# Attention with a decaying complex state and a gated layer on one core: slope clamp dropped, phase turns of two units rounded on ScalarE, new positions for many steps

## The chip, the cores and the metric

The kernel runs on one core of a Trainium2 chip. That core has TensorE (PE; PEld is its weight load), VectorE (DVE), ScalarE (ACT), GpSimd (POOL) and SyncE (SP), whose queue issues nearly all DMAs here. The metric is the device time of one execution in microseconds (us), lower is better.

## The reference

For every batch `b` (4), head `h` (8) and step `t` (768) a 48 x 48 state is turned and decayed by a complex number per row, a product of `k` and `v` is added to its real part, and `q` reads it. The result, 3072 tokens of 384 numbers, goes through a gated layer of width 2048.

```python
mag = np.sqrt(a_re * a_re + a_im * a_im)
scale = np.minimum(mag, 0.999) / (mag + 1e-06)
...
    new_re = ar * S_re - ai * S_im
    new_im = ar * S_im + ai * S_re
    S_re, S_im = (new_re + kv, new_im)
    y[:, :, t] = np.einsum('bhd,bhde->bhe', q[:, :, t], S_re)
...
h = x @ w_in
sp = np.where(h > 20.0, h, np.log1p(np.exp(np.minimum(h, 20.0))))
g = h * np.tanh(sp)
return (g @ w_out).astype(np.float32)
```

## The kernel before, in words

**Units.** The tokens are cut into 12 units of 256 steps (three to a batch), a unit into two chunks of 128. Each unit goes through three stages.

**Elementwise (`ew_steps`).** From `a_re` and `a_im` (tiles `R`, `I`) come the running log magnitude (a scan on DVE, line 333) and the running phase (scans, line 347). The slope `I = a_im * X1` (line 306) is clamped to -1.5..1.5 (line 307), and `test` (line 312) counts whether every ratio is small enough; if not, a flag at the end sends the program to a general path. The phase is brought to one turn in `phi2`: the number of turns `n` as an integer (line 352, DVE), then a subtraction (line 353). ScalarE's exponentials (line 123) and arctangents and sines (line 143) need two tables, so `with_trig` fences the second kind between two table loads (line 131). `grow` multiplies `q` and `k` by the magnitudes (POOL for most units), `rot` by cosine and sine (line 397), and `relay` sends the results through 12 small DMAs per unit from SP into tiles `T` with heads side by side (line 388). Tile `T` has three buffers, one per chunk. Units 0 and 1 work on one chunk at a time, later units on both at once.

**Attention (`attn_steps`), chunk by chunk on PE.** `pkn` transposes the keys (ScalarE copies them to `kn`, line 460), `pa` multiplies keys by queries (DVE masks it into `am`, line 470), `ypsum` gathers `am` times `V` and the old state, `pd` is the chunk's addition to the state (DVE, lines 501 and 503), and `S` times the chunk's last magnitude ends the update (line 505, DVE in unit 0, then POOL). ScalarE copies `ypsum` to `y` (line 488), four DMAs `xf<-y` (line 516) turn it, and `split` makes `xH` and `xL` of it.

**Gated layer (`moe_steps`).** Per pair `j` of eight, 18 matmuls `ph` (line 543), a chain of four activations and DVE steps from `e` to `gh` and `gl`, and later 12 matmuls `po` (line 571). Every product is made of three, with high and low parts of both sides. The weights come in as 64-bit numbers and are converted on the way in 24 pieces of 512 columns (`convert`): ScalarE takes the low words (line 123, `raw<-raw` or `wraw<-wraw`), DVE builds the high words (lines 190 and 194), POOL adds (line 199), ScalarE or DVE copies the high part (line 157) and DVE subtracts (line 158). Pieces named `raw` become `wi`, pieces named `wraw` become `wo`.

**Order.** Each step has a position in the plan, counted in pairs (`EW`, `AT`, `WP`, `LD` for loads, `MB` for the two halves of the layer; `ES`, `TS`, `WS` shift the priority against the position). A scheduler takes the steps by these numbers and lays down one fixed order per engine, and each engine and SP's queue then work strictly in that order. `after` and the numbers `CGA`, `CGN`, `LG` add edges: here the low words of the weights must follow certain trigonometric activations, and `LG = -1` makes the loads of unit 2 wait for the last relay of unit 1. `warm` issues 18 matmuls on a mask (`junk`, line 432) as soon as the first phase is there.

Of the kernel before, what the change touches and what calls it, by code (L numbers as in the profile page):

```python
# [14 lines left out]
F32 = mybir.dt.float32  # L15
# [15 lines left out]
UNITS = B * NU  # L31
# [5 lines left out]
NPAIR = DF // (2 * P)  # L37
# [5 lines left out]
GATE = -1  # L43
GRP = 2
RG, QG, GN = 5, 1, 0
SQ0, SORD, CGA, CGN, CGD, ACTG = 1, 0, 3, 3, 0, 0
YDVE = []
RQ = [(), ()]
LG, WG = -1, 12
W1 = 0  # L50
ADDV = 12
CLAMPP, MAGP = 0, 0
ROTU = 2
ROTP = [2]
# [12 lines left out]
FAST = [0, 1]
EW = [(-16.31, -10.95), (-12.73, -8.83), (-13.6, -11.78), (-17.21, -10.84), (-16.32, -10.6)]
AT = [(-7.75, -4.28), (-4.18, -0.81), (-7.43, -2.2), (-9.42, -3.06), (-10.26, -2.73)]
WP = [(-7.98, -3.45), (-3.03, 2.5), (2.11, 8.49), (9.4, 9.68)]  # L70
WS = [-3.58, -0.64, -1.09, 0.24]
ES = [2.49, -0.99, -0.86, 1.6]
TS = [-0.14, -1.22, 2.46, -0.05]
MB = [-1.35, -0.11]
WL1 = -1.83
RB = 2
XB = 2
LD = [(-17.86, -16.7, -16.5), (-19.19, -20.26, -20.22), (-17.97, -17.71, -17.6), (-21.41, -14.83, -16.39), (-24.18, -15.85, -17.38)]
WL = 512
XRUNS = ((0, 0, 0, 32), (0, 1, 32, 16), (64, 1, 64, 16), (0, 2, 80, 32))  # L80
LOW, HIGH, FADED = 0.55, 2e6, 1e-17
INV2PI = 1.0 / (2.0 * math.pi)
# [4 lines left out]
def tile_kernel(ctx, tc, q, k, v, are, aim, w_in, w_out, out):  # L87
    nc = tc.nc
# [3 lines left out]
    ew = ctx.enter_context(tc.tile_pool(name="ew", bufs=1))  # L92
# [74 lines left out]
    turned = []  # L167
# [13 lines left out]
    def convert(n, raw, dst, ws, raw_is_in=False):  # L181
        u = raw.bitcast(U32).rearrange("p (n two) -> p n two", two=2)
        lo, hi = u[:, :, 0], u[:, :, 1]
        if not TRUNC:
            ins = act(lo.bitcast(I32), lo, AF.Copy, scale=2.0 ** -29)
            if CGA < 9:
                after(ins, trig[0 if len(converted) < CGN else CGA])
            converted.append(ins)
        x = me.tile([P, ws], U32, tag="wx", name="wx", bufs=WXB)
# [40 lines left out]
    def ew_steps(u):  # L230
# [51 lines left out]
        def alloc():  # L282
            if u == 0:
                st["X1"] = at.tile(T4, F32, tag="y", name="X10", bufs=1)
                st["X"] = at.tile(X5, F32, tag="T", name="X0", bufs=TB)
            else:
                st["X1"] = ew.tile(T4, F32, tag="X1", name="X1", bufs=XB)
                st["X"] = ew.tile(X5, F32, tag="X", name="X", bufs=XB)

        def size(g):  # L290
# [13 lines left out]
        def slope(g):  # L304
            R, I, X1, x2, x3 = get(g)
            (nc.gpsimd if 0 < u <= MULP else nc.vector).tensor_tensor(I, I, X1, ALU.mult)
            (nc.gpsimd if 0 < u <= CLAMPP else nc.vector).tensor_scalar(I, I, -1.5, 1.5, ALU.max, ALU.min)
            act(x2, x2, AF.Ln, scale=4.0, bias=tiny)

        def test(g):  # L310
# [38 lines left out]
        def phi2(g):  # L349
            R, I, X1, x2, x3 = get(g)  # L350
            n = I.bitcast(I32)
            nc.vector.tensor_scalar(n, X1, INV2PI, None, ALU.mult)
            turned.append(nc.vector.scalar_tensor_tensor(I, X1, INV2PI, n, ALU.mult, ALU.subtract))
            if g != 0 and uu + 1 < NU:
                nc.vector.tensor_copy(ncar, st["I"][:, NCH - 1, :, C - 1])
# [81 lines left out]

    def attn_steps(u):
# [8 lines left out]
        def chunk(c):  # L447
# [26 lines left out]
            def yv(g):  # L474
                def f():
# [54 lines left out]
    def moe_steps(st, row0, unit=UNITS, cut=False, act=act):  # L530
# [29 lines left out]
        def mm2(j):  # L560
            def f():
# [30 lines left out]
    plan = []  # L592
# [9 lines left out]
    for u in range(NUN):  # L602
# [45 lines left out]
def general(tc, nc, q, k, v, are, aim, pools, moe_steps, split):  # L648
# [162 lines left out]
```

## Time and profile before

| | |
|---|---|
| median of 3 runs | 655.73 us (652.61 to 659.77) |
| profiled execution | 653.54 us, span 651.7 us, mean granted clock 0.944 |
| PE busy | 581.7 us, 89% of the span, 4468 matmuls |
| DVE busy | 502.1 us, 77% |
| ACT busy | 489.2 us, 75%, 45 table loads |
| POOL busy | 127.5 us, 20% |
| first attention matmul | 27.55 us |
| last matmul begins | 645.20 us |

The page cuts the span into 40 slices of 16.3 us. PE is at 9 tenths or more in nearly all slices from the thirteenth on, and mostly below that in the twelve before; the granted clock (PEclk) is below full speed only in those first twelve. A busy share is an average over stages with different limits, so the stages are read apart below.

### The profile page before, as it was taken

How to read it: one execution, taken by the hardware profiler on the slowest of the kernel's cores; microseconds unless marked ns; L12 is line 12 of the kernel's file. 1: busy time of each engine (PE TensorE's matmuls, PEld its weight loads, DVE VectorE, ACT ScalarE, POOL GpSimd, SP SyncE). 2: the span in 40 equal slices, each digit the busy share in tenths (PEclk: the TensorE clock that was granted, in tenths of full speed). 3: DMA queues.
4: the chain of work that ended last, by engine and by line, in shares of the span. 5: the costliest groups of instructions: out<-in, count | busy, mean ns of one | idle time of the engine just before them, and what ended most of it. 6: DMA issues, size and time to landing. Idle time of an engine off the chain costs nothing.

```text
span 651.7 us, 11747 instructions
## 1 busy us (share of the span) xinstructions
PE 581.7 (89%) x4468; PEld 554.5 (85%) x4468; DVE 502.1 (77%) x875; ACT 489.2 (75%) x785; POOL 127.5 (20%) x101
## 2 busy tenths in 40 slices
PE   0686956698689999999999999999999999999996
PEld 0475846598579999999989999999899999999995
DVE  6968989999848869878869868978788796544552
ACT  7857967797757778887988977977888878645661
POOL 2316257435201112002003003003012030000000
PEclk9856888599779999999999999999999999999999
DMA  8765723612840270260460530621711602201000
GB/s 303 219 238 142 245 82 101 190 33 85 210 144 13 87 191 5 89 179 1 117 153 25 143 101 26 183 63 29 192 49 49 171 2 83 64 26 25 1 26 29
DMA packets 58528, 67.05 MB, mean 103 GB/s; under 512 B 4960, under 2 KB 51040, under 8 KB 58464
## 3 DMA queue, kind: packets, MB, share of 16 engines
q1 hardware_dynamic: 58464, 66.23, 35.1%
q8 instruction: 37, 0.61, 0.4%
q14 instruction: 27, 0.22, 0.1%
HBM read 36.96 MB, written 5.51 MB: 65 GB/s over the span
## 4 chain that ended last, share of the span: by engine, by line
PE 38%; DVE 23%; ACT 18%; DMA 7%; issue 7%; SPq 5%; POOL 2%; DVEq 0%; POOLq 0%; ACTq 0%
PE ph L543 14%; PE po L571 13%; ACT e L123 6%; ACT L131 4%; PE pa L467 4%; PE ypsum L483 4%; DVE e L548 3%; DMA R<-a_re 3%; ACT X L123 3%; SPq L388 3%; DVE gl L158 3%; DMA T<-QK 3%; DVE X L347 2%; PE pd L497 2%; DVE R L333 2%
## 5 line engine op out<-in xcount | busy, mean ns | idle before, releaser
L571 PE MATMUL po<-wo,gh 128*128 128x384 f32 x768 | 221.0, 348 | 16.8 <-DVE wo L157 6.0
L543 PE MATMUL ph<-xH,wiH 128*128 128x256 f32 x576 | 169.3, 295 | 10.4 <-ACT xH L157 9.6
L543 PE MATMUL ph<-xL,wiH 128*128 128x256 f32 x576 | 167.3, 291 | 3.1 <-DVE xL L158 3.1
L543 PE MATMUL ph<-xH,wiL 128*128 128x256 f32 x576 | 167.7, 291 | 0.9 <-DVE wiL L158 0.9
L571 PEld LDWEIGHTS po<-wo,gh 128*128 128x128 f32 x768 | 141.6, 190 | 22.5 <-DVE wo L157 6.7
L123 ACT ACTIVATE e<-e 128x512 f32<-128x512 f32 x192 | 119.7, 629 | 50.8 <-DVE e L548 48.9
L571 PE MATMUL po<-wo,gl 128*128 128x384 f32 x384 | 131.3, 342 | 0.0
L543 PEld LDWEIGHTS ph<-xH,wiH 128*128 128x128 f32 x576 | 113.4, 197 | 14.4 <-ACT xH L157 10.4
L543 PEld LDWEIGHTS ph<-xL,wiH 128*128 128x128 f32 x576 | 113.4, 197 | 4.1 <-DVE xL L158 4.1
L543 PEld LDWEIGHTS ph<-xH,wiL 128*128 128x128 f32 x576 | 113.5, 197 | 1.1 <-DVE wiL L158 1.1
L505 POOL TENSOR_TENSOR S<-S,T 96x384 f32<-96x384 f32 x18 | 27.6, 1533 | 314.7 <-DVE S L503 110.3
L553 DVE SCALAR_TENSOR_TENSOR g<-e,ph 128x512 f32<-128x512 f32 x96 | 65.3, 680 | 22.2 <-ACT e L123 21.3
L548 DVE TENSOR_SCALAR e<-e 128x512 f32<-128x512 f32 x96 | 55.9, 583 | 31.5 <-ACT e L123 31.3
L158 DVE TENSOR_TENSOR gl<-g,gh 128x512 fp32r<-128x512 f32 x96 | 75.0, 781 | 1.6
L123 ACT ACTIVATE e<-ph 128x512 f32<-128x512 f32 x96 | 56.5, 591 | 24.6 <-PE ph L543 24.4
L571 PEld LDWEIGHTS po<-wo,gl 128*128 128x128 f32 x384 | 73.1, 190 | 0.4 <-issue 0.4
L123 ACT ACTIVATE e<-e,fifth 128x512 f32<-128x512 f32 x96 | 69.1, 720 | 1.8
L157 DVE CAST gh<-g 128x512 fp32r<-128x512 f32 x96 | 41.0, 427 | 34.3 <-PE po L571 32.6
L131 ACT ACT_TABLE_LOAD x45 | 57.7, 1283 | 1.6 <-PEq L767 0.8
L375 POOL TENSOR_TENSOR QK<-QK,X 128x1536 f32<-128x1536 f32 (+1 forms) x12 | 40.5, 3377 | 76.8 <-ACT X L123 73.2
L467 PE MATMUL pa<-T 96*128 96x128 f32 x384 | 52.9, 288 | 0.6 <-DVE am L470 0.6
L467 PEld LDWEIGHTS pa<-T 96*128 96x128 f32 x384 | 49.5, 203 | 1.2 <-DVE am L470 0.8
(89 smaller groups left out, 820.8 us busy)
## 6 DMA issues: line engine op xcount, KB each, us to landing
T<-X SPq DMA_DIRECT2D x72, 129.0 KB, 2.5
T<-QK SPq DMA_DIRECT2D x72, 129.0 KB, 3.3
raw<-w_in SPq DMA_DIRECT2D x12, 512.0 KB, 9.2
wraw<-w_out SPq DMA_DIRECT2D x12, 512.0 KB, 4.4
QK<-q SPq DMA_DIRECT2D x12, 384.0 KB, 4.3
QK<-k SPq DMA_DIRECT2D x12, 384.0 KB, 5.1
V<-v SPq DMA_DIRECT2D x12, 384.0 KB, 4.6
out_dram<-o SPq DMA_DIRECT2D x24, 192.0 KB, 1.9
```

What stands on the lines that cost most here:

```text
L123: ins = nc.scalar.activation(out, in_, func, **kw)
L131: ins = nc.scalar.preload_act_table_set(name)
L157: heng(h, src)
L158: leng(out=lo, in0=src, in1=h.bitcast(F32), op=ALU.subtract)
L375: (nc.vector if g in FAST and u == 0 else nc.gpsimd).tensor_tensor(QK[..., :C], QK[..., :C], X[..., :C], ALU.mult)
L467: nc.tensor.matmul(pa[:, i, :], st["T"][c][:, 4 * g + i, 1, :C], st["T"][c][:, 4 * g + i, 0, :C], start=True, stop=True)
L483: nc.tensor.matmul(py[64 * par:64 * par + D, i, :], lhs, rhs, start=n == 0, stop=first or n == 1)
L505: (nc.vector if u < WIDE else nc.gpsimd).tensor_tensor(nS, nS, pe, ALU.mult)
L543: nc.tensor.matmul(ph[:, a, :], wi[wp][:, j, kt, a * P:a * P + P], st[xp][:, kt, :], start=n == 0, stop=n == 8)
L548: nc.vector.tensor_scalar_min(e, e, math.exp(20.0))
L553: nc.vector.scalar_tensor_tensor(g, e, 2.5, ph, ALU.subtract, ALU.mult)
L571: nc.tensor.matmul(po[t], gp[:, a, tsl], wo[part][:, wp, 2 * i + a, :], start=j in starts and a == 0 and n == 0, stop=j + 1 in ends and a ...
```

## The change

1. The clamp of the slope goes; `test` still counts the same ratios.
2. In units 0 and 1 the integer number of turns is made by ScalarE (`NACT = 2`, a copy with a scale and an integer output) and not by DVE.
3. In the last pair of the last unit the 12 `po` matmuls run all of the first 128 tokens and then all of the second, where they alternated.
4. The 18 `junk` matmuls stay, and a second batch of 12 is placed after the copy of unit 0's second chunk.
5. Edges: `CGA = 9` drops the edge that held the low words behind the trigonometric activations; `LG = 12` drops the wait of unit 2's loads. `MULP = 0` moves unit 1's slope product from POOL to DVE.
6. New positions and shifts for many steps, and `SHIFT` for four single ones.

```diff
-SQ0, SORD, CGA, CGN, CGD, ACTG = 1, 0, 3, 3, 0, 0
+SQ0, SORD, CGA, CGN, CGD, ACTG = 1, 0, 9, 3, 0, 0
-LG, WG = -1, 12
+LG, WG = 12, 12
-CLAMPP, MAGP = 0, 0
+NACT, MAGP = 2, 0
-FIN0 = -3.39
+FIN0 = -3.09
-MULP = 1
+MULP = 0
-NWARM, WREP, WK = 2, 9, -9.4
+WREP, WREP2, WK = 18, 12, -8.6
-EW = [(-16.31, -10.95), (-12.73, -8.83), (-13.6, -11.78), (-17.21, -10.84), (-16.32, -10.6)]
-AT = [(-7.75, -4.28), (-4.18, -0.81), (-7.43, -2.2), (-9.42, -3.06), (-10.26, -2.73)]
+EW = [(-16.09, -10.95), (-12.73, -8.83), (-13.6, -11.78), (-17.88, -11.79), (-16.56, -10.6)]
+AT = [(-7.62, -4.55), (-3.79, -0.81), (-8.05, -2.82), (-8.41, -3.06), (-10.49, -2.73)]
...
+SHIFT = {32: -0.19, 113: 0.04, 229: 0.63, 252: 0.1}
...
             (nc.gpsimd if 0 < u <= MULP else nc.vector).tensor_tensor(I, I, X1, ALU.mult)
-            (nc.gpsimd if 0 < u <= CLAMPP else nc.vector).tensor_scalar(I, I, -1.5, 1.5, ALU.max, ALU.min)
...
-            nc.vector.tensor_scalar(n, X1, INV2PI, None, ALU.mult)
+            if u < NACT:
+                nc.scalar.activation(n, X1, AF.Copy, scale=INV2PI)
+            else:
+                nc.vector.tensor_scalar(n, X1, INV2PI, None, ALU.mult)
...
+    def spin(count, prev):
+        def f():
             junk = ps.tile([P, 512], F32, tag="po", name="junk", bufs=2)
+            for _ in range(count):
...
+                        if u == 0 and c == 1:
+                            copied.append(ins)
...
-                for a in range(2):
-                    for t in range(2):
+                order = [(a, t) for a in range(2) for t in range(2)]
+                if unit == UNITS - 1 and j + 1 == NPAIR:
+                    order.sort(key=lambda at: at[1])
+                for a, t in order:
...
+    plan.append((WK, len(plan), spin(WREP, turned)))
+    if WREP2:
+        plan.append((FIN0 + 0.01, len(plan), spin(WREP2, copied)))
```

Three places in the order of the instructions are spoken of below.

**ScalarE at the start, unit 0.** `X<-R` are the exponentials of the scanned magnitudes (two per chunk), `raw` the low words of the first weight pieces, `I<-I` the arctangents, `I_105<-X_115` the new integer turns. Before:

```order
L123 ACTIVATE X_116<-X_116 128x3x128 x3
L123 ACTIVATE X_116<-R_104 128x3x128 x4
L131 ACT_TABLE_LOAD
L143 ACTIVATE I_105<-I_105 128x384
L123 ACTIVATE raw_98<-raw_98 128x512
L143 ACTIVATE I_105<-I_105 128x384
L123 ACTIVATE raw_98<-raw_98 128x512 x2
L143 ACTIVATE X_115<-I_105 128x384
```

Now:

```order
L124 ACTIVATE X_116<-X_116 128x3x128 x3
L124 ACTIVATE raw_98<-raw_98 128x512
L124 ACTIVATE X_116<-R_104 128x3x128 x2
L124 ACTIVATE raw_98<-raw_98 128x512
L124 ACTIVATE X_116<-R_104 128x3x128 x2
L132 ACT_TABLE_LOAD
L144 ACTIVATE I_105<-I_105 128x384 x2
L124 ACTIVATE raw_98<-raw_98 128x512 x2
L353 ACTIVATE I_105<-X_115 128x384
L124 ACTIVATE raw_98<-raw_98 128x512
L353 ACTIVATE I_105<-X_115 128x384
L144 ACTIVATE X_115<-I_105 128x384
```

Two weight pieces now stand ahead of the exponentials, and the two turns stand ahead of the first sine.

**VectorE in unit 1's elementwise stage, beside unit 0's attention; then POOL at the weights.** `am`, `S<-pd` and `S<-S,T` belong to unit 0 and wait for PE; `R<-X` and `R<-rmask,R` are unit 1's magnitudes and their scan. VectorE before:

```order
L470 TENSOR_TENSOR am<-pa,cmask 128x512
L503 TENSOR_TENSOR S<-pd,S 96x192 x2
L333 SCALAR_TENSOR_TENSOR R<-rmask,R 128x384
L329 SCALAR_TENSOR_TENSOR R<-X 128x384
L505 TENSOR_TENSOR S<-S,T 96x384
L333 SCALAR_TENSOR_TENSOR R<-rmask,R 128x384
```

Now:

```order
L329 SCALAR_TENSOR_TENSOR R<-X 128x384
L333 SCALAR_TENSOR_TENSOR R<-rmask,R 128x384
L476 TENSOR_TENSOR am<-pa,cmask 128x512
L513 TENSOR_TENSOR S<-S,T 96x384
L333 SCALAR_TENSOR_TENSOR R<-rmask,R 128x384
L511 TENSOR_TENSOR S<-pd,S 96x192 x2
```

POOL, before and now:

```order
L199 TENSOR_TENSOR wraw<-wraw 128x512 x2
L505 TENSOR_TENSOR S<-S,T 96x384
L199 TENSOR_TENSOR wraw<-wraw 128x512
L505 TENSOR_TENSOR S<-S,T 96x384
L199 TENSOR_TENSOR wraw<-wraw 128x512
```

```order
L200 TENSOR_TENSOR wraw<-wraw 128x512 x2
L513 TENSOR_TENSOR S<-S,T 96x384
L200 TENSOR_TENSOR wraw<-wraw 128x512 x2
L513 TENSOR_TENSOR S<-S,T 96x384
L200 TENSOR_TENSOR wraw<-wraw 128x512
```

Both scans now stand ahead of the additions to the state, the first also ahead of the last mask; on POOL the fourth weight piece stands ahead of the second `S`.

**PE where unit 2's attention ends and unit 3's begins.** `ypsum` are unit 2's last outputs, `pkn` the first transposes of unit 3's keys. Before:

```order
L483 MATMUL ypsum<-am,V 48x128 x2
L483 MATMUL ypsum<-T,S 48x128 x2
L459 MATMUL pkn<-ident,T 128x96 x8
L483 MATMUL ypsum<-am,V 48x128 x2
L483 MATMUL ypsum<-T,S 48x128 x2
L483 MATMUL ypsum<-am,V 48x128 x2
```

Now:

```order
L489 MATMUL ypsum<-am,V 48x128 x2
L489 MATMUL ypsum<-T,S 48x128 x2
L489 MATMUL ypsum<-am,V 48x128 x2
L489 MATMUL ypsum<-T,S 48x128 x2
L489 MATMUL ypsum<-am,V 48x128 x2
L465 MATMUL pkn<-ident,T 128x96 x8
```

Unit 2's outputs are now complete ahead of the transposes. On SP's queue the order of later units is changed too: in five of the eight units 4 to 11 all six `T<-X` and two `T<-QK` went out ahead of the four `xf<-y` of the unit before, in the other three five `T<-X`; now all eight send five `T<-X`, then `xf<-y`, then the rest.

## Rows read from the trace of the kernel before

**Rows 1.** Busy us by stage: start:end, length, PE, PEld, DVE, ACT, POOL, clock, DMA, GB/s.

```profile
36.00:52.00 16.00, 10.63 (x73) 9.66 (x72) 7.81 (x20) 10.20 (x20) 4.63 (x6) 0.61 0.62 203
52.00:60.00 8.00, 6.61 (x29) 6.31 (x30) 7.27 (x16) 6.21 (x12) 5.71 (x2) 0.51 0.29 93
60.00:165.00 105.00, 82.69 (x585) 76.35 (x584) 100.69 (x162) 80.07 (x125) 51.32 (x30) 0.85 0.42 130
165.00:190.00 25.00, 15.31 (x104) 13.46 (x103) 16.31 (x31) 14.88 (x28) 2.98 (x3) 0.79 0.72 190
190.00:645.60 455.60, 451.74 (x3611) 438.45 (x3610) 339.19 (x584) 350.96 (x552) 52.16 (x39) 1.00 0.28 76
```

**Rows 2.** Timeline of ScalarE: start, length, instruction, count [idle before it, releaser].

```profile
11.34 0.94 ACT L123 ACTIVATE X<-R 128x384 f32<-128x384 f32 x2 [1.04 <-DVE R L333]
```

**Rows 3.** Timeline of SP's queue; then DMA issues, the first weight load: KB, us to landing.

```profile
5.24 4.56 SPq L175 DMA_DIRECT2D raw<-w_in  x6
...
raw<-w_in SPq DMA_DIRECT2D x1, 512.0 KB, 8.0
```

**Rows 4.** Timelines of VectorE and ScalarE, unit 1's scan.

```profile
40.91 0.69 DVE L470 TENSOR_TENSOR am<-pa,cmask 128x512 f32<-128x512 f32 x1 [1.07 <-PE pa L467]
43.66 0.95 DVE L333 TENSOR_TENSOR_SCAN R<-rmask,R 128x384 f32<-128x384 uint8 x1
...
44.64 0.94 ACT L123 ACTIVATE X<-R 128x384 f32<-128x384 f32 x2 [3.62 <-DVE R L333]
```

**Rows 5.** VectorE: a turn, unit 2's clamp; all clamps (ns: least, median, most).

```profile
16.58 0.36 DVE L352 TENSOR_SCALAR I<-X 128x384 int32<-128x384 f32 x1
79.56 1.19 DVE L307 TENSOR_SCALAR I<-I 128x768 f32<-128x768 f32 x1
...
L307 DVE TENSOR_SCALAR I<-I x14: 336/550/1202, 7.2 to 508.0; 128x768 f32<-128x768 f32 x10, 128x384 f32<-128x384 f32 x4
```

**Rows 6.** Timelines of POOL, ScalarE and VectorE around unit 1's state products.

```profile
78.84 1.49 POOL L505 TENSOR_TENSOR S<-S,T 96x384 f32<-96x384 f32 x1 [6.44 <-DVE S L503]
...
87.76 6.80 POOL L505 TENSOR_TENSOR S<-S,T 96x384 f32<-96x384 f32 x1 [3.35 <-DVE S L503]
...
95.59 0.65 ACT L157 CAST wo<-wraw 128x512 fp32r<-128x512 f32 x1 [5.93 <-POOL wraw L199]
...
96.27 0.69 DVE L158 TENSOR_TENSOR wo<-wraw,wo 128x512 fp32r<-128x512 f32 x1 [2.41 <-ACT wo L157]
```

**Rows 7.** Timelines of PE and SP's queue, from unit 2's end to its layer.

```profile
175.10 1.51 PE L459 MATMUL pkn<-ident,T 96*128 96x96 f32 x8 [6.44 <-DMA T<-QK]
180.01 4.55 SPq L516 DMA_DIRECT2D xf<-y  x4
187.04 0.58 PE L543 MATMUL ph<-xH,wiH 128*128 128x256 f32 x1 [2.90 <-ACT xH L157]
```

**Rows 8.** PE's timeline, first filler and first layer matmuls; then pieces of the chain.

```profile
17.68 6.31 PE L432 MATMUL junk<-cmask 128*128 128x512 bf16 x18 [17.68 <-DVE I L353]
52.89 0.80 PE L543 MATMUL ph<-xH,wiH 128*128 128x256 f32 x2 [6.26 <-ACT xH L157]
...
123.68 4.14 PE ph L543 x18
542.17 2.12 PE ph L543 x18
```

**Rows 9.** PE's waits from 190 to 640 us: us, times, longest; then timelines.

```profile
PE pkn L459 <- DMA T<-QK: 3.7, 3, 1.3
...
320.76 0.57 ACT L488 COPY y<-ypsum 112x512 f32<-112x512 f32 x1
318.41 3.21 SPq L388 DMA_DIRECT2D T<-X  x5
321.73 2.54 SPq L516 DMA_DIRECT2D xf<-y  x4
```

**Rows 10.** ScalarE's timeline at the end.

```profile
645.05 1.02 ACT L586 ACTIVATE o<-po 128x384 f32<-128x384 f32 x2 [7.23 <-PE po L571]
```

More of the change, by code (lines that the diff above doesn't have):

```diff
@@ L55 @@
 TREE = 1
-WXB, WRB, WI = 1, 2, 512
-FIN0 = -3.39
+WRB, WI = 2, 512
+FIN0 = -3.09
 FS = 0.0
@@ L62 @@
 SUBP = 0
-MULP = 1
+MULP = 0
 LONG = 2
 WIDE = 1
-NWARM, WREP, WK = 2, 9, -9.4
+WREP, WREP2, WK = 18, 12, -8.6
 FAST = [0, 1]
-EW = [(-16.31, -10.95), (-12.73, -8.83), (-13.6, -11.78), (-17.21, -10.84), (-16.32, -10.6)]
-AT = [(-7.75, -4.28), (-4.18, -0.81), (-7.43, -2.2), (-9.42, -3.06), (-10.26, -2.73)]
[L70 to L74, printed above, removed]
+EW = [(-16.09, -10.95), (-12.73, -8.83), (-13.6, -11.78), (-17.88, -11.79), (-16.56, -10.6)]
+AT = [(-7.62, -4.55), (-3.79, -0.81), (-8.05, -2.82), (-8.41, -3.06), (-10.49, -2.73)]
+WP = [(-7.98, -3.4), (-2.51, 2.77), (1.94, 7.2), (9.3, 9.35)]
+WS = [-3.58, -1.77, 0.05, 1.02]
+ES = [3.85, -0.83, -1.67, 1.33]
+TS = [0.58, -1.31, 2.46, -0.05]
+MB = [-1.21, -0.14]
 WL1 = -1.83
+SHIFT = {32: -0.19, 113: 0.04, 229: 0.63, 252: 0.1}
 RB = 2
-XB = 2
-LD = [(-17.86, -16.7, -16.5), (-19.19, -20.26, -20.22), (-17.97, -17.71, -17.6), (-21.41, -14.83, -16.39), (-24.18, -15.85, -17.38)]
+XB, X1B = 2, 2
+LD = [(-17.86, -17.24, -16.49), (-18.78, -19.85, -19.81), (-17.97, -17.71, -17.6), (-21.23, -15.07, -17.56), (-24.18, -15.85, -17.38)]
 WL = 512
@@ L188, in convert @@
             converted.append(ins)
-        x = me.tile([P, ws], U32, tag="wx", name="wx", bufs=WXB)
+        x = me.tile([P, ws], U32, tag="wx", name="wx", bufs=1)
         first = nc.vector.tensor_scalar(x, hi, 3, 0x3FFFFFF8, ALU.logical_shift_left, ALU.bitwise_and)
@@ L286, in alloc @@
             else:
-                st["X1"] = ew.tile(T4, F32, tag="X1", name="X1", bufs=XB)
+                st["X1"] = ew.tile(T4, F32, tag="X1", name="X1", bufs=X1B)
                 st["X"] = ew.tile(X5, F32, tag="X", name="X", bufs=XB)
@@ L426, in ew_steps @@
         return steps
-    def warm():
-        for i in range(NWARM):
+    copied = []
+    def spin(count, prev):
+        def f():
             junk = ps.tile([P, 512], F32, tag="po", name="junk", bufs=2)
-            for _ in range(WREP):
+            for _ in range(count):
                 ins = nc.tensor.matmul(junk, cmask, cmask.unsqueeze(1).broadcast_to([P, 4, P]), start=True, stop=True)
-                tc.add_manual_dep(ins.ins, turned[0].ins.name,
+                tc.add_manual_dep(ins.ins, prev[0].ins.name,
                                   mybir.DependencyInfo(mybir.DependencyClass.Sync, mybir.DependencyReason.DATA), reason="clock")
+        return f
     state = {}
@@ L487, in f @@
                             st["y"] = at.tile([112, 4, TU], F32, tag="y", name="y", bufs=1)
-                        (nc.vector.tensor_copy if u < 1 and c in YDVE else nc.scalar.copy)(st["y"][:, :, cs], py)
+                        ins = (nc.vector.tensor_copy if u < 1 and c in YDVE else nc.scalar.copy)(st["y"][:, :, cs], py)
+                        if u == 0 and c == 1:
+                            copied.append(ins)
                 return f
@@ L624, in tile_kernel, with due @@
             place([f(n * half + m) for m in range(n)], *WP[2 * half + i], WS[2 * half + i])
-    rank = {x[:2]: i for i, x in enumerate(sorted(plan, key=lambda x: (x[3] if len(x) > 3 else x[0], x[1])))}
+    def due(x):
+        key = x[1] if x[1] < edge else 1000 + x[1] - edge
+        return (x[3] if len(x) > 3 else x[0]) + SHIFT.get(key, 0.0), x[1]
+    rank = {x[:2]: i for i, x in enumerate(sorted(plan, key=due))}
     for x in sorted(plan, key=lambda x: x[:2]):
@@ L665, in general @@
     w2 = io.tile([P, 2, BJ, D], F32, tag="QK", name="w2", bufs=1)
-    w3 = ew.tile([P, BJ, D], F32, tag="X1", name="w3", bufs=XB)
+    w3 = ew.tile([P, BJ, D], F32, tag="X1", name="w3", bufs=X1B)
     kv, t1, t2, t3, t4 = w1[:, 0], w1[:, 1], w2[:, 0], w2[:, 1], w3
```

3 lines of the change are left out of this document (1 added, 2 removed).

## The prediction, made before the changed kernel had run

> **What bounds the kernel now.** I read the page's slices first: they split the span into a ragged first part and a full second one. The stage table then puts numbers on it. From 190 us to the last matmul PE is busy 451.74 of 455.60 us at the full clock [rows 1]: what is done there must be done by PE, and only its 3.9 us of idle time could go. The 165 us before are a ramp. From 36 to 52 us no engine is full: PE runs at a granted clock of 0.61 and VectorE is busy 7.81 of 16 us [rows 1]. From 60 to 165 us VectorE is busy 100.69 of 105 us [rows 1], because it converts the weights, serves the first units' layer and prepares later units all at once; PE idles 22.3 us there. From 165 to 190 us PE idles 9.7 and VectorE 8.7 us [rows 1]: there both wait for something else. So the reader should see that a change pays if it starts the VectorE-bound stretch earlier, shortens it, or closes the hole at 165 to 190 us. After 190 us it can hardly pay, but it can cost.
>
> **The change part by part.** The sum is made against the profiled execution, 653.54 us (span 651.7); the median of the runs shown, 655.73 us, lies 2.2 us above it, and I add that at the end.
>
> *Low words of weights at the start, +0.9 us.* ScalarE was free at 11.34 - 1.04 = 10.30 us and got the first exponentials at 11.34 [rows 2]. Now a `raw` piece stands in between. Its load was issued at 5.24 us and took 8.0 us [rows 3], so it landed at 13.2 us; it now goes out ahead of one V load, which at most brings it forward by about 1 us (an estimate: 384 KB at the rate at which the 512 KB pieces follow each other). So the exponentials start 1.5 to 2.6 us late. Later ScalarE gets back two conversions that no longer stand between arctangents and sines, but makes two turns at about 0.45 us; VectorE loses two clamps and two turns of 0.36 us [rows 5] there. I take +0.9 us for the first attention matmul, bounds 0 and +2.5.
>
> *Unit 1's scan out of the queue, -3.5 us.* ScalarE waited 3.62 us for the scan at 43.66 us [rows 4]. The scan stood behind a mask that waited 1.07 us for PE [rows 4] and behind unit 0's state additions. Its own input was ready before, so it can run about 4 us earlier, less the 0.9 above, and with it unit 1's sines, rotations and relays. VectorE's idle 8.2 us between 36 and 52 us [rows 1] is what this is paid from. Unit 0's copy `y` stands between unit 1's arctangents and turns on ScalarE now, so part may be lost to that wait. Since VectorE is the bound right after, an earlier start is worth its full amount. Bounds: 0 and -5.
>
> *Clamps and turns in the ramp, -0.9 us.* The clamps of units 2 and 3 lie in the VectorE-bound stretch; unit 2's took 1.19 us where the median is 0.55 [rows 5]. Unit 1's slope comes back from POOL as two products (by the 0.69 us of a 512-wide one [rows 4], some 0.5 us each), which eats what its own clamps and turns free. From 190 us on, the clamps lie beside a full PE and are worth nothing. The long clamp ran beside a POOL product that began at 78.84 and took 1.49 us [rows 6]. So I count the clamps at some 0.47 us each, -0.9 us, with -1.9 us at the long durations as one end and 0 as the other. *The Trainium skill, SBUF — State Buffer, section "Who interferes with whom", says that such a VectorE operation and a POOL operation that reads SBUF lock a port pair against each other for a whole instruction, whichever starts second waiting. By that the extra 0.6 us was POOL's, and the next VectorE operation would inherit it: it speaks against the -1.9 end. The trace agrees in so far as the same clamp has durations from its median to 1202 ns.*
>
> *POOL's weight piece ahead of the state product, -2.4 us.* The product at 87.76 us took 6.80 us; the weight piece behind it kept ScalarE waiting 5.93 and VectorE 2.41 us [rows 6]. With the piece ahead, VectorE's 2.41 us is what the bounding engine gains. Bounds 0 (another wait there) and -5.9.
>
> *Unit 2's outputs ahead of unit 3's transposes, -5 us.* PE waited 6.44 us at the transposes for unit 3's relays, with unit 2's last outputs behind them; only after those came `xf<-y` at 180.01 and the first matmul of unit 2's layer at 187.04 us [rows 7]. Without that the outputs are done some 7 us earlier. But SP's queue sends unit 3's relays and loads ahead of `xf` in either order, and the wait for the relays stays, so not all is won: of the 9.7 us of PE's idle time in that stage [rows 1] I take half. Bounds 0 and -9.
>
> *Second filler, -0.5 us.* The first 18 took 6.31 us, 0.35 each; 12 are 4.2 us, in a gap that was 6.26 us before [rows 8] and that I expect shorter, so up to +1.5 us could stick out. What it may give is the clock: from 52 to 60 us, after that gap, the granted clock was 0.51 [rows 1], that is 1.2 GHz, where 18 matmuls cost 4.14 us against 2.12 us at 2.4 GHz [rows 8]. Some 30 matmuls make -3 us at best. But those matmuls feed ScalarE and VectorE, which are late next. Hence -0.5.
>
> *Relays of later units, +1.2 us.* From 190 us on PE waited three times for `T<-QK`, 3.7 us in all [rows 9], in just those three of the eight units whose queue sends `xf<-y` after five `T<-X`. Now all eight do. Five more waits of 1.24 would be +6.2 us; none at all would be -3.7; PE's order around the transposes is new too. I take the middle.
>
> *Last matmuls by halves, 0.* ScalarE takes the two results at 645.05 us in 1.02 us [rows 10]; the second half still ends last. At best -0.5.
>
> Sum: 0.9 - 3.5 - 0.9 - 2.4 - 5.0 - 0.5 + 1.2 = -10.2 us, so 643.3 us against the profiled time and **645.5 us** as a median. A measurement of this kernel tells about 1% (6.6 us) from no change.
>
> **The rivals.**
>
> *VectorE stays the bound and nothing arrives (about 654.5 us).* For it: 100.69 of 105 us. If unit 1's head start is eaten by other steps in VectorE's order, and unit 2's values are late for another reason, only clamps and the POOL piece are left: 0.9 - 0.9 - 2.4 + 1.2 = -1.2 us. Against it: VectorE's idle time before 52 us and after 165 us is real.
>
> *The ramp closes (about 633 us).* All far ends but the filler's at once, with the start still at +0.9: -5 - 1.9 - 5.9 - 9 - 3 + 1.2 + 0.9 = -22.7 us, 633 us as a median; less if the clock stays up longer, as it was only 0.85 from 60 to 165 us [rows 1]. Against it: the terms share VectorE. *The Trainium skill, TensorE: Matmul & The Clock Gate, "What's actually happening", has the slow clock as the default and activity as what releases it; by that, fewer holes pay twice, which is this rival. The trace agrees: at 123.68 us matmuls after waits took twice the time of those at 542.17 [rows 8].*
>
> *Relays behind the copy of `y` (slower, about 664 us).* In the new queue order `xf<-y` waits for ScalarE's copy with the sixth `T<-X` and all `T<-QK` behind it, in every unit. In the unit shown the copy ended at 321.33 and the fifth `T<-X` was issued at 321.62 us [rows 9]: a margin of 0.3 us. Each us by which copies are later costs PE, which has no slack, eight us. It decides from a lateness of 1.7 us: 8 x (1.24 + 1.7) - 3.7 = +19.8, with the other terms' -11.4 that is +8.4 us, 664 us as a median. Against it: the copies stand early on ScalarE, and PE's own order makes them.
>
> **How the numbers follow.** The forecast gets 0.59, the closed ramp 0.13, the VectorE bound 0.20, the relays 0.08. The forecast's own range is 640 to 651 us. 8 times in 10 the time should lie from 636 to 657 us: this leaves out most of the closed ramp and the relays. Faster by over 1% means below 649.2: the closed ramp and most of the forecast, 0.62. Within 1%: the rest of the forecast and the VectorE bound, 0.28. Slower: 0.10.
>
> **What would show it.** In the profile after: the first transposes near 28.4 us with ScalarE idle before its first `raw` piece; unit 1's scan near 40 us and its table load before the sines near 45 us; no wait of ScalarE for POOL near 90 us; unit 2's outputs without a hole and the first matmul of its layer near 175 us; from there the same 456 us. I am wrong if VectorE is as full but no earlier, if PE's waits at later transposes grow past 10 us, or if the first transposes come after 30 us.

## The result, and the profile after

The changed kernel takes 647.22 us (median of 6 runs, 646.06 to 649.71), the kernel before 656.53 us in the same comparison: a ratio of 0.987 [0.983, 0.991]. The forecast was 645.5 us. The profiled execution took 646.22 us with a span of 644.4, against 653.54 and 651.7 before.

I read the same stages as in [rows 1]:

```profile
36.00:52.00 16.00, 15.31 (x88) 11.22 (x86) 12.29 (x27) 11.49 (x23) 7.30 (x7) 0.54 0.67 220
52.00:60.00 8.00, 4.74 (x27) 4.12 (x27) 8.00 (x13) 6.72 (x12) 3.36 (x3) 0.86 0.73 227
60.00:165.00 105.00, 82.09 (x605) 75.28 (x606) 103.79 (x162) 78.65 (x121) 43.13 (x27) 0.86 0.43 124
165.00:190.00 25.00, 20.27 (x158) 19.43 (x154) 18.23 (x35) 19.27 (x34) 2.57 (x2) 0.93 0.55 145
190.00:638.00 448.00, 443.64 (x3541) 428.96 (x3539) 328.37 (x566) 346.49 (x541) 56.70 (x39) 1.00 0.29 76
```

VectorE does 12.29 instead of 7.81 us of work before 52 us and is then as full as before or fuller. PE idles as long from 60 to 165 us (22.9 us against 22.3); the hole at 165 to 190 us is half as large. The last stage has PE as full as it was.

A chain of milestones shows better where the gain lies. The timelines of ScalarE and PE at the start, to be read beside [rows 2, 3]:

```profile
11.60 0.66 ACT L124 ACTIVATE raw<-raw 128x512 int32<-128x512 uint32 x1 [1.45 <-DMA raw<-w_in]
12.16 0.92 ACT L124 ACTIVATE X<-R 128x384 f32<-128x384 f32 x2
...
27.07 0.85 PE L465 MATMUL pkn<-ident,T 96*128 96x96 f32 x8 [1.71 <-DMA T<-QK]
```

The exponentials start 0.8 us later, and still the first transposes come at 27.07 instead of 27.55 us. Unit 0's relays are not what came earlier: their first `T<-QK` goes out at 23.17 us, before at 23.07. The transposes come 3.9 us behind it instead of 4.5. Unit 1, beside [rows 4], on VectorE, ScalarE and SP's queue:

```profile
39.42 0.95 DVE L333 TENSOR_TENSOR_SCAN R<-rmask,R 128x384 f32<-128x384 uint8 x1
...
40.40 0.94 ACT L124 ACTIVATE X<-R 128x384 f32<-128x384 f32 x2 [0.86 <-DVE R L333]
43.53 1.28 ACT L132 ACT_TABLE_LOAD   x1
...
47.01 0.59 ACT L494 COPY y<-ypsum 112x512 f32<-112x512 f32 x1 [0.69 <-PE ypsum L489]
...
56.00 1.86 SPq L391 DMA_DIRECT2D T<-QK  x3
```

The same relays of units 1 and 3 on SP's queue before:

```profile
58.92 1.86 SPq L388 DMA_DIRECT2D T<-QK  x3
...
168.41 4.21 SPq L388 DMA_DIRECT2D T<-QK  x6
```

The scan is 4.2 us earlier, unit 1's first `T<-QK` 2.9 us. In between, ScalarE waits for unit 0's copy `y` at 47.01. From unit 1's first `T<-QK` to unit 3's it takes 107.1 us (56.00 to 163.06), before 109.5 (58.92 to 168.41). PE's waits in that stretch (us in total, times, longest), and the weight piece beside [rows 6] on POOL and ScalarE:

```profile
PE po L581 <- DVE wo L158: 10.4, 1, 10.4
PE ph L551 <- DVE g L561: 3.6, 4, 1.4
...
PE po L581 <- ACT wo L158: 3.4, 1, 3.4
```

```profile
82.84 4.30 POOL L200 TENSOR_TENSOR wraw<-wraw 128x512 int32<-128x512 int32 x1 [4.79 <-ACT wraw L124]
87.11 1.02 POOL L513 TENSOR_TENSOR S<-S,T 96x384 f32<-96x384 f32 x1
...
87.18 0.65 ACT L158 CAST wo<-wraw 128x512 fp32r<-128x512 f32 x1 [2.27 <-POOL wraw L200]
```

The product that took 6.80 us takes 1.02, but now the piece ahead of it takes 4.30: the long instance has passed to the operation that stands first. Unit 2's end, beside [rows 7]:

```profile
163.06 4.11 SPq L391 DMA_DIRECT2D T<-QK  x6
172.16 2.57 SPq L524 DMA_DIRECT2D xf<-y  x4
...
169.54 0.85 PE L465 MATMUL pkn<-ident,T 96*128 96x96 f32 x8 [3.55 <-DMA T<-QK]
180.53 1.16 PE L473 MATMUL pa<-T 96*128 96x128 f32 x8 [1.17 <-ACT kn L466]
```

`xf<-y` comes 9.1 us behind unit 3's relays, before 11.6. Unit 2's layer starts at 181.45 us (187.04 in [rows 7]). PE's waits from 190 to 640 us, and ScalarE's last copy, beside [rows 9, 10]:

```profile
PE pkn L465 <- DMA T<-QK: 4.4, 6, 1.0
...
638.14 0.49 ACT L596 ACTIVATE o<-po 128x384 f32<-128x384 f32 x1 [0.39 <-PE po L581]
```

The last copy ends 7.4 us earlier (638.63 against 646.07). The gain by place: 2.9 us until unit 1's relays, 2.4 from there to unit 3's, 2.5 at unit 2's outputs, and 0.4 given back by the end. In a second profile of the same kernel (648.02 us, below) these parts are 1.5, 2.8 and 3.1 us, and 2.1 given back: a single part is known to 1 or 2 us only.

### The profile page after: what moved, and what is told of

Its sections match the earlier page's. It is cut to its first block, busy times and chain, and to the rows that moved or that the text cites. A ratio compares the mean times of both kernels' runs of the same rounds, so it can differ in the third digit from the quotient of the medians.

```text
span 644.4 us, 11738 instructions
## 1 busy us (share of the span) xinstructions
PE 579.0 (90%) x4480; PEld 547.3 (85%) x4480; DVE 500.3 (78%) x859; ACT 493.4 (77%) x789; POOL 124.2 (19%) x99
## 4 chain that ended last, share of the span: by engine, by line
PE 36%; DVE 27%; ACT 17%; DMA 9%; issue 6%; SPq 4%; POOL 1%; DVEq 0%; ACTq 0%; POOLq 0%
PE po L581 14%; PE ph L551 13%; ACT e L124 7%; DVE gl L159 3%; ACT L132 3%; PE ypsum L489 3%; DVE e L556 3%; PE pa L473 3%; DMA T<-QK 3%; SPq L391 3%; ACT X L124 2%; DMA R<-a_re 2%; PE pd L505 2%; DVE g L561 2%; DMA xf<-y 2%
## 5 line engine op out<-in xcount | busy, mean ns | idle before, releaser
L551 PE MATMUL ph<-xL,wiH 128*128 128x256 f32 x576 | 165.1, 287 | 4.4 <-DVE xL L159 4.4
L551 PE MATMUL ph<-xH,wiL 128*128 128x256 f32 x576 | 165.5, 288 | 0.0
L581 PEld LDWEIGHTS po<-wo,gh 128*128 128x128 f32 x768 | 141.4, 190 | 18.4 <-DVE wo L158 10.7
L551 PEld LDWEIGHTS ph<-xH,wiH 128*128 128x128 f32 x576 | 111.5, 194 | 8.4 <-issue 4.8
L551 PEld LDWEIGHTS ph<-xL,wiH 128*128 128x128 f32 x576 | 111.5, 194 | 5.3 <-DVE xL L159 5.2
L551 PEld LDWEIGHTS ph<-xH,wiL 128*128 128x128 f32 x576 | 111.3, 193 | 0.2 <-issue 0.2
L158 DVE CAST gh<-g 128x512 fp32r<-128x512 f32 x96 | 42.8, 445 | 33.9 <-PE po L581 32.6
L473 PE MATMUL pa<-T 96*128 96x128 f32 x384 | 51.4, 283 | 4.5 <-DVE S L511 3.4
```

Of the source, the lines that this page charges most:

```text
L158: heng(h, src)
L473: nc.tensor.matmul(pa[:, i, :], st["T"][c][:, 4 * g + i, 1, :C], st["T"][c][:, 4 * g + i, 0, :C], start=True, stop=True)
L551: nc.tensor.matmul(ph[:, a, :], wi[wp][:, j, kt, a * P:a * P + P], st[xp][:, kt, :], start=n == 0, stop=n == 8)
```

## The experiments

The scheduler lays a new order down for any edit. To change one thing alone, each kernel below has the order of every engine written out: a table, and from each instruction an edge that adds no wait to the one before it on its engine. With nothing else edited that is the changed kernel's program, instruction for instruction. Times are medians of 6 runs, where nothing else is said; ratios are to the kernel before, which ran beside all of them (medians of 654.83 to 654.93 us). The changed kernel was run again, beside three of them (ScalarE's first pieces, POOL's order, POOL's large products): 647.91 us (643.71 to 648.96), ratio 0.989 [0.985, 0.993].

> The changed kernel once more, as the measure for the kernels beside it: 646.5 to 648.5 us under every theory.

**The code edits undone in the new order.**

```diff
+            nc.vector.tensor_scalar(I, I, -1.5, 1.5, ALU.max, ALU.min)
-NACT, MAGP = 2, 0
+NACT, MAGP = 0, 0
-WREP, WREP2, WK = 18, 12, -8.6
+WREP, WREP2, WK = 18, 0, -8.6
```

> The changed kernel with every engine's order written out as the scheduler made it, and in it the clamps (behind each slope product, 14 on VectorE), the turns of units 0 and 1 (four, on VectorE) put back and the 12 matmuls of the second filler left out. Theory 'the order': the new order carries the gain, the code edits about 1 us (0.9 for clamps and turns, 0.5 for the filler): 647.5 to 649.5 us, ratio to the kernel before 0.986 to 0.990. Rival 'the code': without the edits most of the gain is gone: 652 us or more, ratio above 0.993.

Measured: 647.92 us, ratio 0.989 [0.985, 0.992]. The order carries the gain; the edits together are worth less than the runs can tell. In the trace the way from unit 1's relays to unit 3's is 107.9 us (58.05 to 165.97), 0.9 to 1.2 more than in the changed kernel's two profiles (107.1 and 106.7). Unit 1's relays start at 58.05 us, there at 56.00 and 57.41; those two differ by 1.4 us, so what the edits give ahead of the relays can't be read off.

**Without the second filler** (`WREP2 = 0`).

> The changed kernel in its own order without the 12 filler matmuls behind unit 0's copy of y. Theory 'paid back': the clock from 52 to 60 us falls to about 0.5 again and the 18 matmuls of the first pair take about 2 us longer, but PE then waits less for unit 0's low halves (2.4 us at 57.4 in the changed kernel): 646.5 to 648 us. Rival 'the clock pays': 649 us or more. Third: the filler only stands in the way of the first pair: 645.5 us or less.

Measured: 646.13 us (644.01 to 647.98), ratio 0.986 [0.982, 0.990]: between the first and the third case, and no slower. The clock from 52 to 60 us is 0.50 instead of 0.86, PE waits 4.8 us for `xH` ahead of the pair and 2.1 for `xL` in it, and the way from unit 1's relays to unit 3's is 107.0 us, the same. As far as these runs tell, the filler pays for a clock that nobody uses there.

**Unit 2's outputs behind unit 3's transposes again.**

```diff
 L489 MATMUL ypsum<-am,V 48x128 x2
 L489 MATMUL ypsum<-T,S 48x128 x2
+L465 MATMUL pkn<-ident,T 128x96 x8
 L489 MATMUL ypsum<-am,V 48x128 x2
 L489 MATMUL ypsum<-T,S 48x128 x2
 L489 MATMUL ypsum<-am,V 48x128 x2
-L465 MATMUL pkn<-ident,T 128x96 x8
```

> The changed kernel in its own order, but on PE the eight transposes of unit 3's keys stand ahead of the last six matmuls of unit 2's outputs, as they did in the kernel before. Theory 'the hole': the transposes wait for unit 3's relays at about 170 us and the outputs behind them, so xf<-y goes out 4 to 8 us later than 172.2 and unit 2's layer starts at 183 to 187 instead of 178.2 us: 652 to 655 us. Rival 'late values': the outputs' own operands are late in any case, the layer starts within 1 us of before: 647 to 648 us.

(The 178.2 us in this text was a misreading; unit 2's layer starts at 181.45 us.) Measured: 649.95 us (12 runs, 646.59 to 655.14), ratio 0.994 [0.991, 0.996]. SP's queue in its profile:

```profile
162.51 3.80 SPq L450 DMA_DIRECT2D T<-QK  x6
...
173.24 2.60 SPq L583 DMA_DIRECT2D xf<-y  x4
```

`xf<-y` comes 10.7 us behind the relays instead of 9.1, and unit 2's layer starts at 183.10. From the relays to the start of the last copy it is 477.4 us, against 475.1 and 476.1 in the two profiles of the changed kernel, and the medians differ by 2.0 to 2.7 us: the hole is real, but worth some 2 us, less than half of what the first theory said.

**Unit 1's scans late again.**

```diff
-L333 TENSOR_TENSOR_SCAN R<-rmask,R
 L476 TENSOR_TENSOR am<-pa,cmask
 L513 TENSOR_TENSOR S<-S,T
-L333 TENSOR_TENSOR_SCAN R<-rmask,R
 L511 TENSOR_TENSOR S<-pd,S x2
+L333 TENSOR_TENSOR_SCAN R<-rmask,R
 L513 TENSOR_TENSOR S<-S,T
+L333 TENSOR_TENSOR_SCAN R<-rmask,R
```

> The changed kernel in its own order, but on VectorE unit 1's scans stand behind unit 0's two additions to the state, as in the kernel before. Theory 'head start': the scan runs about 4 us later (43.5 instead of 39.4 us), unit 1's sines and relays 3 us later, and the VectorE-bound stretch starts and ends that much later: 649.5 to 650.5 us. Rival 'VectorE eats it': the steps behind are full in any order, and by 165 us nothing is left: 647 to 648 us.

Measured: 649.64 us (11 runs, 644.82 to 653.01), ratio 0.993 [0.989, 0.996], so about 2 us slower, as the first theory said. But in the profiled execution (645.12 us) the scan ran at 39.47 us all the same, and `T<-QK` of unit 1 came at 54.78, earlier than in the changed kernel. What differs is PE's clock (the figure behind POOL's busy time, in a table by 4 us with the columns of [rows 1]). The changed kernel, then this one:

```profile
28.00:32.00 4.00, 1.73 (x16) 1.54 (x14) 4.00 (x9) 4.00 (x10) 1.23 (x1) 1.00 0.79 213
32.00:36.00 4.00, 3.92 (x32) 3.61 (x32) 4.00 (x10) 2.85 (x6) 0.00 (x0) 0.73 1.10 354
36.00:40.00 4.00, 4.00 (x25) 3.54 (x24) 2.40 (x7) 1.45 (x3) 0.00 (x0) 0.50 1.03 374
40.00:44.00 4.00, 4.00 (x27) 3.33 (x27) 2.90 (x6) 2.91 (x6) 2.53 (x1) 0.50 0.74 298
```

```profile
28.00:32.00 4.00, 1.64 (x17) 1.45 (x17) 4.00 (x9) 4.00 (x9) 1.23 (x1) 1.00 0.83 220
32.00:36.00 4.00, 4.00 (x46) 3.52 (x47) 4.00 (x9) 3.02 (x7) 0.00 (x0) 1.00 1.11 345
36.00:40.00 4.00, 4.00 (x49) 3.64 (x49) 3.90 (x10) 1.08 (x3) 0.00 (x0) 1.00 0.99 367
40.00:44.00 4.00, 0.83 (x16) 0.57 (x12) 1.89 (x5) 3.54 (x6) 2.49 (x4) 1.00 0.95 384
```

At 2.4 GHz PE is through with unit 0's attention by about 41 us, at 1.2 GHz by 47 us. With the fast clock the additions to the state that the scan stands behind are early too, and its place costs nothing. The times of its runs fit this: the three with a mean granted clock of 0.965 to 0.968 took 644.8 to 647.6 us, the six at 0.951 to 0.954 took 649.5 to 653.0, where the changed kernel's three at 0.952 to 0.954 took 648.0 to 649.7. So with the slow clock the place would cost some 2 us; no profile shows such a run. The nearly equal beginning (1.64 and 1.73 us of work between 28 and 32) leads to either.

**ScalarE's first two weight pieces late again** (behind unit 0's arctangents).

> The changed kernel in its own order, but on ScalarE the first two raw pieces stand behind unit 0's arctangents, as in the kernel before. Theory 'the piece costs the start': the exponentials start at 10.2 us instead of 12.16, the first transposes come 1 to 1.5 us earlier than 27.07, the end 1 to 1.5 us earlier than the changed kernel's. Rival 'paid by the weights': the first transposes come earlier too, but the weight pieces are converted later on POOL and VectorE, and the end is the same within 0.7 us or later. Third: the first transposes don't move at all, because something else releases unit 0's relays.

Measured: 647.15 us (643.68 to 648.15), ratio 0.988 [0.985, 0.992]. The exponentials start at 10.71 us, the first transposes at 26.79 against 27.07 and 26.95: the third case, though not for its reason. Of ScalarE's head start of 1.4 us 0.3 are left at unit 0's relays (`T<-QK` at 22.91 against 23.17 us). ScalarE in the changed kernel and in this one:

```profile
14.48 1.28 ACT L132 ACT_TABLE_LOAD   x1
...
17.71 0.51 ACT L353 ACTIVATE I<-X 128x384 int32<-128x384 f32 x1
```

```profile
13.11 1.28 ACT L192 ACT_TABLE_LOAD   x1
...
17.42 0.53 ACT L413 ACTIVATE I<-X 128x384 int32<-128x384 f32 x1
```

The two pieces have moved from ahead of the exponentials to behind the arctangents, but there they still stand ahead of the turns `I<-X`. So ScalarE works them off before the turns in either order, and the head start goes into them.

**POOL's product ahead of the weight piece again.**

```diff
+L513 TENSOR_TENSOR S<-S,T 96x384
 L200 TENSOR_TENSOR wraw<-wraw 128x512
-L513 TENSOR_TENSOR S<-S,T 96x384
```

> The changed kernel in its own order, but on POOL the second product of unit 1's state stands ahead of the fourth weight piece, as in the kernel before. Theory 'POOL's order was worth 2.4 us': PE's wait for ScalarE's wo (3.4 us at 87.9) grows by 2 to 4 us and the end is 1.5 to 3 us later than the changed kernel's. Rival 'only the name of the wait changed': the weight piece was long (4.3 us) in either order because it runs beside VectorE, the wait is 3 to 5 us either way, and the end moves by less than 1 us.

Measured: 647.11 us (644.06 to 648.67), ratio 0.988 [0.985, 0.992]: the rival. PE's wait for ScalarE's `wo` is 4.3 instead of 3.4 us, from unit 1's relays to unit 3's it takes 107.3 us, the same. The piece did not stay long, as the rival had it:

```profile
86.23 2.36 POOL L573 TENSOR_TENSOR S<-S,T 96x384 f32<-96x384 f32 x1 [6.42 <-DVE I L404]
88.56 1.03 POOL L260 TENSOR_TENSOR wraw<-wraw 128x512 int32<-128x512 int32 x1
```

What the profiles have in common is VectorE beside it: POOL's long operation ends 0.6 to 0.8 us after a VectorE scan or product with two inputs that closes a row of them (87.96 and 88.59 here, 86.30 and 87.14 in the changed kernel, 87.68 and 88.51 in its second profile, 93.87 and 94.56 before). So VectorE's order would set that end, and not POOL's; this is read from four traces and not tested.

**POOL's large products on VectorE.** In the changed kernel, VectorE and POOL beside unit 2's and unit 3's products:

```profile
91.92 5.21 DVE L159 TENSOR_TENSOR xL<-xf,xH 128x256 fp32r<-128x256 f32 x3
145.16 3.46 DVE L358 COPY ncar<-I 128x3 f32<-128x3 f32 x1
...
93.19 3.66 POOL L378 TENSOR_TENSOR QK<-QK,X 128x1536 f32<-128x1536 f32 x1
144.46 4.15 POOL L378 TENSOR_TENSOR QK<-QK,X 128x1536 f32<-128x1536 f32 x1 [6.42 <-ACT X L124]
```

A copy of three columns takes 3.46 us and ends at 148.62 us, POOL's product at 148.61. *The Trainium skill, SBUF — State Buffer, section "Who interferes with whom", says that such a copy, or a VectorE operation with two inputs in SBUF, and a POOL operation that reads SBUF can shut each other out for a whole instruction; the trace agrees, as the two end within 0.01 us.* VectorE is the bound here, so the experiment asks what POOL's help costs:

```diff
-            (nc.vector if g in FAST and u == 0 else nc.gpsimd).tensor_tensor(
+            (nc.vector if u < 4 else nc.gpsimd).tensor_tensor(
                 QK[..., :C], QK[..., :C], X[..., :C], ALU.mult)
```

> The changed kernel in its own order, with the products QK<-QK,X of units 1, 2 and 3 on VectorE instead of POOL (unit 1's two behind the additions to the state, unit 2's behind the three xL, unit 3's ahead of the copy ncar). Theory 'VectorE pays for POOL's product': the three xL take 1.3 instead of 5.2 us and ncar 0.2 instead of 3.5 us, against 1.8 us for each product; unit 1's two take 0.95 each instead of 2.68 and 2.13. VectorE gains 3.6 us between 60 and 165 us, the end comes 2.5 to 4.5 us earlier than the changed kernel's: 643 to 645 us. Rival 'the lengths have another cause' (the operations wait for their own operands): they stay long, VectorE has 3.6 us more to do, the end is 3 to 4 us later: 650 to 651 us.

Measured: 644.48 us (639.91 to 645.34), ratio 0.984 [0.980, 0.988], 3.4 us less than the changed kernel beside it. VectorE's timeline now:

```profile
93.33 1.72 DVE L219 TENSOR_TENSOR xL<-xf,xH 128x256 fp32r<-128x256 f32 x3
94.97 1.75 DVE L438 TENSOR_TENSOR QK<-QK,X 128x1536 f32<-128x1536 f32 x1
...
144.66 1.75 DVE L438 TENSOR_TENSOR QK<-QK,X 128x1536 f32<-128x1536 f32 x1
146.33 0.18 DVE L418 COPY ncar<-I 128x3 f32<-128x3 f32 x1
```

The way from unit 1's relays to unit 3's is 103.3 us, 3.4 less than the 106.7 of the changed kernel's second profile. Here a microsecond of VectorE was a microsecond of the end.

**Weight casts to ScalarE, on top of that** (`HACT, HMOD = 3, 3`).

> The kernel of grow_dve, and in it the eight casts of weights to their high halves that were on VectorE (one piece in three) on ScalarE, at the same places in time. Six of them lay in the VectorE-bound stretch, 0.41 us each and one 0.77. Theory 'what VectorE is spared between 60 and 165 us comes off the end, one to one, since ScalarE has 26 us of idle time there': 2 to 2.8 us earlier than grow_dve's 644.5: 641.7 to 642.5 us. Rival 'ScalarE's order makes new waits': VectorE waits for casts that stand behind exponentials, 644 to 646 us.

Measured: 643.08 us (641.68 to 646.51), ratio 0.982 [0.978, 0.986]. 101.3 us from relays to relays, 2.1 less; the runs show 1.4 of it.

**PE's holes ahead of 32 us closed, in the changed kernel** (`WREP = 22`, and the order of VectorE):

```diff
 L312 SCALAR_TENSOR_TENSOR X<-R,X
+L476 TENSOR_TENSOR am<-pa,cmask x2
 L303 TENSOR_TENSOR X<-X
 L159 TENSOR_TENSOR wiL<-raw,wiH
 L312 SCALAR_TENSOR_TENSOR X<-R,X
-L476 TENSOR_TENSOR am<-pa,cmask
```

> The changed kernel in its own order, with two holes of PE ahead of 32 us closed: the first filler has 22 matmuls instead of 18, and on VectorE the first two masks am stand right behind the first test of unit 1, three operations earlier, so that PE need not wait 2.3 us for them at 30 to 32 us. Theory 'the hole costs the clock': the granted clock stays at 1.00 from 30 to 42 us where it fell to 0.50 in most profiles, unit 0's attention ends some 4 us earlier, unit 1's relays T<-QK start near 55 us instead of 57.4, and the end comes 1.5 to 2.5 us earlier than the changed kernel's 647.7: 645 to 646.5 us. Rival 'only the hole': PE gains the 2 us, the clock falls all the same, unit 1's relays start at 56.5 to 57.5, the end moves by less than 1 us. Second rival 'VectorE eats it': the relays come early but nothing is left of it at 165 us.

Measured: 645.18 us (642.05 to 646.24), ratio 0.984 [0.980, 0.987], 2 to 2.7 us less. The profiled execution speaks against the theory of the hole: PE did not wait between 28.3 and 40 us, and yet the clock fell at 30 (0.98 from 28 to 30, 0.50 from 30 on; `T<-QK` of unit 1 at 57.06). The other five runs have a mean granted clock of 0.962 to 0.973, the changed kernel's twelve 0.952 to 0.962. So the clock may stay up more often, but not for certain; only the one profile shows where it fell.

**All together, without and with the casts `gh` on ScalarE** (`GACT = 2` in the second).

> All of it together: grow_dve, the weight casts on ScalarE, the masks and the longer first filler of am_early, and also the 16 casts gh of units 0 and 1 on ScalarE, at the same places in time (0.41 us each on VectorE, 12 of them in its bound stretch). Theory 'VectorE's time is the price': grow_hact less 1.5 to 2.5 us for the clock and less 4 to 5 us for the casts: 635 to 637 us. Rival 'ScalarE becomes the bound': it is busy 79 of 105 us there and gets some 12 us more, and each low half gl now waits for ScalarE: 639 to 642 us, with VectorE idle for several us behind ACT between 60 and 165 us.

Measured: 640.16 us (639.20 to 642.29), ratio 0.977 [0.973, 0.981]; the rival's time. VectorE waits for ScalarE now; its waits from 60 to 165 us begin with:

```profile
DVE gl L219 <- ACT gh L218: 3.3, 4, 2.1
DVE g L621 <- ACT e L184: 2.7, 4, 1.3
```

From relays to relays it takes 102.7 us, 1.4 more than in the kernel with the weight casts alone, though VectorE is busy only 96.0 of 105 us. That kernel also lacked the early masks and the longer first filler, so the casts `gh` are not yet shown to be the cause. Hence the last run:

> The kernel of four with the 16 casts gh of units 0 and 1 back on VectorE. Theory 'the casts gh gave nothing, the early masks and the longer filler gave all': in four the way from unit 1's relays to unit 3's took 102.7 us, in grow_hact 101.3, with VectorE waiting 8.2 us for ScalarE; so this kernel is as fast as four or up to 1.5 us faster: 638.5 to 640.5 us. Rival 'the casts gave part of it': 641 to 643 us, and the way from unit 1's relays to unit 3's is no shorter than 102.5 us.

Measured: **638.67 us** (637.28 to 641.59), ratio 0.976 [0.973, 0.979], faster than both kernels. The time is as the theory said, but the way from unit 1's relays (at 52.67 us) to unit 3's is 102.5 us, as long as with the casts `gh`. So those lengthened nothing and gave nothing: VectorE's spared time went into its waits. The 1.5 us between the two medians are within the spread of the runs. Why the way is 1.2 us longer than with the weight casts alone, where unit 1's relays start 5 us later, stays open. PE's clock in this execution (same columns):

```profile
32.00:36.00 4.00, 3.95 (x42) 3.46 (x40) 4.00 (x10) 3.66 (x8) 0.00 (x0) 1.00 1.09 336
36.00:40.00 4.00, 3.23 (x44) 2.90 (x46) 4.00 (x9) 2.44 (x6) 1.30 (x1) 1.00 0.99 376
40.00:44.00 4.00, 0.45 (x10) 0.20 (x4) 3.50 (x10) 3.97 (x8) 2.30 (x4) 1.00 0.96 382
```

## Why the prediction was right, and where it was not

The time and the frame were right: VectorE bounds the stretch from 60 us to unit 3's relays, PE the rest, and what comes early to unit 3's relays comes off the end. Against a sum of -10.2 us the profiles show -7.4 (-5.3 with the changed kernel's second profile). That the time came within 1.7 us of the forecast is partly luck: POOL's piece and unit 2's outputs, -7.4 in the sum, gave some 2 us by the experiments, while the start cost nothing and the way between the relays got 1.6 us shorter by the order alone (109.5 to 107.9), which belongs to no step that was tested. By its terms:

- *Low words at the start, +0.9.* Wrong in sign, and small. The first piece was ready at 11.6 us, not 13.2 (issued at 4.93 it took 6.6 us, not the 8.0 of [rows 3]), and two pieces fewer ahead of the exponentials move the transposes by 0.2 to 0.3 us, since ScalarE has them to do ahead of the turns all the same. The relays go out 0.1 us later than before; the 0.5 us by which the transposes come earlier lie behind their issue. With a change that lies far behind it (unit 3's transposes) `T<-QK` came at 24.36 us, so the start moves by over 1 us by itself.
- *Unit 1's scan, -3.5.* Right in kind, and somewhat large: the scan came 4.2 us earlier in one profile and 2.8 in the other, the relays 2.9 and 1.5 (the sum had 2.6 with the start), and putting the scans back cost 1.7 to 2.4 us between medians. The named loss to the copy `y` came (0.69 us of waiting). What the step left out is the clock: in the profiles unit 1's relays start at 54.8 to 55.2 us where the clock was up from 36 us on (52.7 and 53.1 in the last two kernels), at 56.0 to 58.1 where it was down. That is as much as the whole term.
- *Clamps and turns, -0.9.* Right as far as the runs tell: 0.9 to 1.2 us on the way from relays to relays, which the medians (647.92 against 647.22 and 647.91) do not resolve.
- *POOL's weight piece, -2.4.* Wrong. The step put VectorE's wait of 2.41 us down to the product's place ahead of the piece. But whichever operation stands first there ends at about the same time (the piece at 88.51 us in the changed kernel's second profile, the product at 88.59 with the swap undone), and undoing the swap lost nothing that can be measured. VectorE's idle time between the relays did fall from 5.1 to 1.0 us, of it the wait for `wo` from 2.4 to 0.4 us, but with the swap undone that wait is 0.4 us too.
- *Unit 2's outputs, -5.* Right in mechanism, too large: some 2 us by the experiment. I gave it half of the stage's 9.7 us of idle time; the wait for the relays (3.55 us) and the 9.1 us from relays to `xf<-y` stayed. The first matmul of that layer came at 181.45, not near 175, for a further reason: PE had unit 1's layer to work off until 179.4 us and then stood 1.17 us at unit 3's `pa`, waiting for a copy `kn` that ScalarE makes behind the casts `xH`, which wait for `xf`.
- *Second filler, -0.5.* Nothing, or a loss of up to 1.8 us between medians whose intervals overlap. The reason given, that the pair feeds engines that are late next, held.
- *Relays of later units, +1.2.* 0.7 us of waits more (4.4 against 3.7), in six waits of at most 1.0 us. The rival of the copy `y` did not come. The order was not quite as stated: seven of the eight units send five `T<-X` ahead of `xf<-y`, unit 4 sends six (from 214.54 us).
- *Last matmuls by halves, 0.* Nothing: from the start of the last matmul to the end of the last copy it was 0.87 us (645.20 to 646.07) and is 0.86 (637.77 to 638.63).

The signs that were asked for: the scan at 39.4 and the table load at 43.5 us came as said, waits at later transposes stayed below 10 us; ScalarE's wait for POOL did not go away (2.27 us), and the first transposes were too early for the step that they were to show.

Of the rivals, "VectorE stays the bound" was half true: it stayed the bound, and the change shortened what it does before. The closed ramp (633) was not reached by any order that was tried; the last experiment comes to 638.67 with less work on VectorE, and in its profile with the clock up. Not tested one by one are the loads of unit 2 without their wait (`LG`) and most of the new positions.

## What to carry to other kernels

Split a ragged kernel by milestones (here the relays of units 1 and 3 and the last copy) and price each step by the stretch in which it lies; two profiles of the same kernel show how far a milestone moves by itself. When one engine bounds a stretch, look at its long instances of short operations first: they can name the engine that holds it up, and taking the work back can be cheaper than the help. A long instance of a short operation is no price of its place in the queue: after a swap the length may pass to the operation that stands there now.

## What the runs showed of the hardware

The granted clock of TensorE between 30 and 44 us differs between executions. In the two profiles of the changed kernel it fell from 1.00 to 0.50 near 34 and near 32 us; in profiles of nearly equal kernels it stayed at 1.00 (the scans late) or had fallen and was back by 36 us (the first pieces late). Unit 1's relays go with it, from 54.8 to 58.1 us. The runs of one kernel spread over up to 8.6 us (646.59 to 655.14 with unit 3's transposes first); what part of that is the clock is not shown. *The Trainium skill, TensorE: Matmul & The Clock Gate, section "What's actually happening", says that what the chip watches runs free of the kernel, so that executions of one kernel differ in when the clock changes; the traces agree, with 34 and 32 us for a fall in the middle of one kernel.* What decides it in this stage stays open: a wait of PE of 2.3 to 2.4 us ahead of it was followed by either, and without that wait the clock fell once in one profile.

POOL's product of 128x1536 f32 takes 3.66 to 4.15 us and holds VectorE up for 3.3 to 3.5 us (the copy 3.46 against 0.18 us without it, the three `xL` 5.21 against 1.72); on VectorE itself it takes 1.75 us.
